# RWKV attention followed by a SwiGLU feed-forward block: a replanned static schedule with one fixed order of DMA issues

## The chip, the cores and the metric

One Trainium2 chip, one of its cores. The metric is the device time of one execution in microseconds (us): the median of repeated runs. A profiled execution adds a span, from the first to the last instruction, and a trace.

## What is computed

The first half is a recurrence over 768 steps for 4 batches of 8 heads with 48 channels:

```python
for t in range(S):
    cur = einsum('bhd,bhe->bhde', u[None] * kt, vt)
    y[:, :, t] = einsum('bhd,bhde->bhe', rt, state + cur)
    state = wt[:, :, :, None] * state + einsum('bhd,bhe->bhde', kt, vt)
```

Its output, 3,072 tokens of 384 channels, goes through a feed-forward network (FFN):

```python
xn = x / sqrt(mean(x * x) + 1e-06) * rms_g
g, val = xn @ w_gate, xn @ w_val            # 384 -> 1536
out = silu(g) * val @ w_out                 # 1536 -> 384
```

## The kernel before

**Tiling.** The 768 steps are cut into six superblocks, SB0 to SB5, of 128 steps. A superblock has four units, one per batch, each 128 tokens by 384 channels. Per unit, four loads of 192 KB bring w, k, r and v. The decays are summed by matmuls with masks (line 650), exponentiated on ScalarE (655) and multiplied into r and k on VectorE (658). The product is transposed, by TensorE (671) in SB0 and SB1 and by a DMA transpose (663) from SB2 on. Then come the scores (687), their mask on VectorE (690), the output (700, 703), the new state (709, 714, 721), the bonus term with u on GpSimd and VectorE (725, 729, 732, 737), the sum (741), the norm (745, 750, 751, 754) and a transpose into the FFN's input xnt (761, 765).

**FFN.** Per superblock, 12 blocks of 512 output columns in PSUM each for gate and value (line 774), silu on ScalarE (778), the product on VectorE (782), and 12 groups of four matmuls with w_out (790), whose result is copied (796, 798) and stored (802). Before the change, SB0 and SB1 run gate and value in two groups of two units (matmuls of 256 columns), the others in one group of four (512 columns). The gate and value weights arrive as 12 loads of 384 KB (606) in 7 staging buffers, 4 of which lie in the second `ht` buffer, and are scaled and cast to bf16 by ScalarE (614, gate) and VectorE (616, value). w_out comes in three DMAs that GpSimd issues (620).

**What sets the order.** Nothing is scheduled on the chip. `program` (line 218) lists every operation with engine, duration, dependences, ring buffers and a priority worked out from six target times `T`, and `Scheduler.run` (63) places them one by one: on each engine, among the operations ready soon, the one of lowest priority number. The order found is then issued as it is; each engine runs its own list in order and waits on semaphores. Loads and stores share the queue of SyncE (SP). Loads after a fixed first list (`LOADS`, 468) go out by priority; `in_w`, `in_rk` and `in_v` have two buffers per superblock parity, so a load for SB m waits until SB m-2 has been read. In the planner a DMA occupies SP for 0.55 us whatever is queued. ScalarE swaps its function table (624) 13 times.

Of the kernel before, what the change touches and what calls it, by code (L numbers as in the profile page):

```python
# [41 lines left out]
class Scheduler:  # L42


    DMA_RATE = {"in": 0.940 / 196608, "w": 1 / 330e3, "out": 0.60 / 196608, "tr": 1.0 / 262144}
# [7 lines left out]
    def op(self, name, eng, busy, fn, deps=(), prio=0.0, lat=0.0, alloc=(), nbytes=None, after=None):  # L53
        o = Op(name, eng, busy, lat, list(deps), prio, fn, [(r, k) for r, k, _ in alloc], nbytes)
# [8 lines left out]
    def run(self):  # L63
# [23 lines left out]
        dma_t = 0.0  # L87
        order = []
# [17 lines left out]
        while len(order) < n:  # L106
# [29 lines left out]
            o.slots = {}  # L136
            for r, k in o.alloc:
# [12 lines left out]
                else:  # L150
# [3 lines left out]
                    o.slots[k] = i  # L154
            o.start = ts
            free[o.eng] = ts + o.busy
            if o.nbytes is not None:
                kind, nb = o.nbytes
                st = max(ts + o.busy + 0.6, dma_t)
                dma_t = st + nb * self.DMA_RATE[kind]  # L160
                o.end = dma_t + 1.3
            else:
                o.end = ts + o.busy + o.lat
# [30 lines left out]
LOOK = 0.03  # L194

# [22 lines left out]
def program(S, T):  # L218
# [13 lines left out]


# [13 lines left out]
    for a, b in zip(LOADS, LOADS[1:]):  # L247
        before[b] = ("ldw",) + a[1:] if a[2] in "gh" else ("ld",) + a
    for m, j, w in seq:
# [43 lines left out]
    for m in range(NSB):  # L293
        t_le = T[0] - 30 if m == 0 else (T[0] + LE1 if m == 1 else T[m - 2] + (T[m - 1] - T[m - 2]) * LEFRAC)
        b = t_le
# [21 lines left out]
        for j in range(SB):  # L317
# [3 lines left out]
            if m == 0 or m == 1 and LE1SPREAD:  # L321
# [38 lines left out]
            S.op(("ruk2",) + u, POOL, 1.04, ("ruk2", m, j), [("ruk1",) + u], z - LAG["xa"] - 4.9, 0.03)  # L360
# [5 lines left out]
            S.op(("sq",) + u, ACT, act_t(DM, False, 0.18), ("x_sq", m, j), [("xa",) + u], z - LAG["sq"], 0.03)  # L366
# [25 lines left out]
    for m in range(NSB):  # L392
# [4 lines left out]
        for gi, (j0, nj) in enumerate(groups[m]):  # L397
            nf = 4 // nj
            nblk = FC // nf
            for i in range(nblk):  # L400
                fs = list(range(i * nf, (i + 1) * nf))
                frac = (i + 0.5) / nblk if INTERLEAVE else (sum(n for _, n in groups[m][:gi]) * 1.0 + nj * i / nblk) / SB
                t = T[m] + dur_gv * frac
                if m == 0:
                    t = T[0] + dur_gv * (i / nblk) + gi * HEADSP * nj
# [4 lines left out]
                xd = [("xe", m, j) for j in range(j0, j0 + nj)]  # L410
                for s, d in zip("gv", wdep):
# [3 lines left out]
                         [("bank", ("gvb", m, gi, i, s), rd)])  # L415
                ph = SIPH(m, gi, i)
# [10 lines left out]
            for j in range(j0, j0 + nj):  # L427
                for q in range(NOQ):
# [6 lines left out]
                    else:  # L435
# [3 lines left out]
                eng = OENG(m, j)  # L439
# [417 lines left out]
```

## Time and profile before

| | |
|---|---|
| median of 3 runs | 274.2 us (273.45 to 274.66) |
| the profiled execution | 271.89 us, span 269.8 us |
| mean granted TensorE clock, share of full | 0.956 |
| TensorE busy (matmuls) | 210.4 us, 78% |
| VectorE busy | 161.8 us, 60% |
| ScalarE busy | 135.0 us, 50% |
| GpSimd busy | 88.8 us, 33% |
| HBM read and written | 26.15 MB and 4.72 MB |

Busy time is a share of the whole span; where the time is lost is read per stretch, by which wait ends last there. In the rows, PE is TensorE, DVE VectorE, ACT ScalarE, POOL GpSimd, and a "q" behind an engine is its queue of DMA issues.

### The profile page before, as it was taken

To read this page: it belongs to the slowest core of one execution; us is meant where nothing else is said; L and a number is where in the kernel's file an instruction comes from. 1 tells how busy PE (TensorE), PEld (TensorE's weight loads), DVE (VectorE), ACT (ScalarE), POOL (GpSimd) and SP (SyncE) were. 2 spreads that over 40 slices of the span, in tenths; PEclk is the share of its full clock that TensorE was granted. 3 is DMA by queue.
4 is the path that set the end of the run, shared out by engine and by line. 5 is a ranking of instruction groups with operands and counts; after the bars stand their busy time and mean duration, and the time that the engine had idled before them with its cause. 6 is when DMAs were issued, how large, how long until landed. Compare 5 with 4: busy or idle time off the path is not lost.

```text
span 269.8 us, 4531 instructions
## 1 busy us (share of the span) xinstructions
PE 210.4 (78%) x1678; PEld 124.3 (46%) x1688; DVE 161.8 (60%) x273; ACT 135.0 (50%) x242; POOL 88.8 (33%) x133
## 2 busy tenths in 40 slices
PE   0476980577759895398989889978988888999984
PEld 0255760255526683185544436533454334554442
DVE  3479743457748572378985787684657647515521
ACT  2559652157163456547844439543486345533420
POOL 2566128634463570047632673120221011110000
PEclk9999999599798999579999999999999999999999
DMA  6999999999999967597999601920005800020002
GB/s 124 192 186 338 212 191 176 262 247 170 190 194 217 194 127 129 108 195 119 207 177 232 87 2 45 163 67 0 2 5 124 148 0 0 4 89 29 2 8 108
DMA packets 127142, 34.18 MB, mean 127 GB/s; under 512 B 117776, under 2 KB 127120, under 8 KB 127120
## 3 DMA queue, kind: packets, MB, share of 16 engines
q1 hardware_dynamic: 124992, 32.52, 64.4%
q0 software_dynamic: 1584, 1.18, 2.8%
q10 hardware_dynamic: 544, 0.20, 0.4%
q8 instruction: 13, 0.21, 0.4%
q14 instruction: 9, 0.07, 0.1%
HBM read 26.15 MB, written 4.72 MB: 114 GB/s over the span
## 4 chain that ended last, share of the span: by engine, by line
PE 44%; DVE 15%; SPq 13%; ACT 10%; DMA 7%; issue 6%; POOL 4%; DVEq 0%; ACTq 0%; POOLq 0%
PE ps L774 20%; PE ps L790 15%; SPq L593 12%; DVE ht L782 8%; ACT sg L778 5%; DMA in_v<-in_v_dram 4%; DMA in_rk<-in_r_dram 2%; PE ps L650 2%; SPq L606 2%; POOL ruk L725 1%; PE ps L687 1%; ACT ps L655 1%; DVE xb L741 1%; DMA in_w<-in_w_dram 1%; ACT vb L632 1%
## 5 line engine op out<-in xcount | busy, mean ns | idle before, releaser
L782 DVE TENSOR_TENSOR ht<-ps,sg 128x512 bf16<-128x512 f32 x72 | 49.2, 690 | 44.8 <-PE ps L774 27.0
L778 ACT ACTIVATE sg<-ps 128x512 bf16<-128x512 f32 x72 | 42.3, 597 | 59.1 <-PE ps L774 34.7
L774 PE MATMUL ps<-xnt,wv 128*128 128x256 bf16 (+1 forms) x286 | 59.9, 334 | 14.5 <-DVE wv L616 8.9
L774 PE MATMUL ps<-xnt,wg 128*128 128x256 bf16 (+1 forms) x280 | 60.1, 336 | 6.3 <-ACT wg L614 1.5
L790 PE MATMUL ps<-wo,ht 128*128 128x384 bf16 x288 | 55.4, 331 | 2.4 <-ACT xnt L765 0.9
L774 PEld LDWEIGHTS <-wv 128*128 128x128 bf16 x288 | 28.2, 100 | 36.8 <-DVE wv L616 11.6
L737 POOL TENSOR_TENSOR ydr<-in_v,diag 128x384 f32<-128x384 f32 x24 | 19.9, 830 | 61.7 <-DVE xb L741 52.9
L774 PEld LDWEIGHTS <-wg 128*128 128x128 bf16 x288 | 27.9, 102 | 24.9 <-issue 7.3
L790 PEld LDWEIGHTS <-ht 128*128 128x128 bf16 x288 | 26.7, 99 | 20.5 <-issue 5.5
L725 POOL TENSOR_TENSOR ruk<-in_rk 128x384 f32<-128x384 f32 x24 | 24.0, 999 | 25.8 <-DMA in_rk<-in_r_dram 23.3
L690 DVE TENSOR_TENSOR qts<-ps,mask_lt 128x1024 bf16<-128x1024 f32 x24 | 29.1, 1220 | 3.6 <-PE ps L687 3.4
L658 DVE TENSOR_TENSOR rkA<-in_rk,ps 128x768 bf16<-128x768 f32 x24 | 22.3, 950 | 13.2 <-ACT ps L655 13.1
L729 POOL TENSOR_TENSOR ruk<-ruk,u_bc 128x384 f32<-128x384 f32 x24 | 24.0, 1000 | 1.2
L655 ACT ACTIVATE ps<-ps 128x768 f32<-128x768 f32 x24 | 18.8, 794 | 9.2 <-PE ps L650 9.1
L750 POOL TENSOR_SCALAR rstd<-rstd 128x1 f32<-128x1 f32 x24 | 4.7, 198 | 53.2 <-ACT junk L745 52.5
L741 DVE TENSOR_TENSOR xb<-ps,ydr 128x384 bf16<-128x384 f32 x24 | 13.3, 554 | 9.8 <-PE ps L703 4.8
L650 PE MATMUL ps<-lw,mask_lt 128*128 128x384 bf16 x24 | 8.8, 366 | 12.8 <-ACT lw L627 7.9
L765 ACT COPY xnt<-ps 128x384 bf16<-128x384 bf16 x24 | 11.4, 480 | 14.7 <-PE ps L761 8.1
L624 ACT ACT_TABLE_LOAD x13 | 16.7, 1283 | 1.9 <-PEq L841 1.7
L732 DVE TENSOR_REDUCE diag<-ruk 128x8 f32<-128x384 f32 x24 | 13.1, 546 | 7.5 <-POOL ruk L729 7.4
L721 DVE TENSOR_TENSOR st<-ps,wcr 48x192 bf16<-48x192 f32 x40 | 14.0, 352 | 3.7 <-PE ps L774 2.3
L745 ACT ACTIVATE junk<-xb 128x384 bf16<-128x384 bf16 x24 | 12.4, 518 | 5.8 <-DVE xb L741 5.6
(49 smaller groups left out, 202.5 us busy)
## 6 DMA issues: line engine op xcount, KB each, us to landing
in_w<-in_w_dram SPq DMA_DIRECT2D x24, 192.0 KB, 4.2
in_rk<-in_k_dram SPq DMA_DIRECT2D x24, 192.0 KB, 4.6
in_rk<-in_r_dram SPq DMA_DIRECT2D x24, 192.0 KB, 4.6
in_v<-in_v_dram SPq DMA_DIRECT2D x24, 192.0 KB, 4.5
out_dram<-obr SPq DMA_DIRECT2D x24, 192.0 KB, 2.1
ht<-in_moe_w_val_dram SPq DMA_DIRECT2D x5, 384.0 KB, 5.0
ht<-in_moe_w_gate_dram SPq DMA_DIRECT2D x3, 384.0 KB, 5.4
stage_x<-in_moe_w_gate_dram SPq DMA_DIRECT2D x3, 384.0 KB, 5.9
```

The lines of the kernel that those rows point to most:

```text
L593: self.nc.sync.dma_start(out=t, in_=getattr(self, w)[j, :, m * L:(m + 1) * L, :].rearrange("h t d -> t h d"))
L624: self.nc.scalar.preload_act_table_set(LN_EXP if ph[0] == "le" else SILU)
L655: self.nc.scalar.activation(out=ps, in_=ps, func=AF.Exp)
L658: self.nc.vector.tensor_tensor(out=self.rkA[:, self.slot["rkA", m, j], :, :, 0:D], in0=self.in_rk[:, self.slot["in_rk", m], j], in1=self.b ...
L690: self.nc.vector.tensor_tensor(out=self.qts[:, self.slot["qts", m, j]].rearrange("p a q t -> p (a q) t"), in0=self.b2(("qb", m, j)).rearra ...
L725: self.nc.gpsimd.tensor_tensor(out=self.ruk[:, self.slot["ruk", m, j]], in0=rk[:, 0], in1=rk[:, 1], op=ALU.mult)
L729: self.nc.gpsimd.tensor_tensor(out=t, in0=t, in1=self.u_bc, op=ALU.mult)
L737: self.nc.gpsimd.tensor_tensor(out=self.ydr[:, self.slot["ydr", m, j]], in0=self.in_v[:, self.slot["in_v", m], j], in1=self.diag[:, m * SB ...
L774: self.nc.tensor.matmul(ps[:, i * n:(i + 1) * n], lhsT=w[:, c, f * 128:(f + 1) * 128], rhs=x[:, c], start=(i == 0 and c == 0), stop=(i == ...
L778: self.nc.scalar.activation(out=self.sg[:, self.slot[("sg",) + key]], in_=self.b1(("gvb",) + key + ("g",)), func=AF.Silu)
L782: self.nc.vector.tensor_tensor(out=self.ht[:, self.slot["ht", m], fs[0]:fs[-1] + 1, j0 * L:j0 * L + n], in0=self.b1(("gvb",) + key + ("v", ...
L790: self.nc.tensor.matmul(ps, lhsT=self.ht[:, self.slot["ht", m], f, j * L:(j + 1) * L], rhs=self.wo[:, f, :], start=(f == 0), stop=(f == FC ...
```

## The change

It replaces the planner's rules and its numbers; no arithmetic of the result changes.

- **One DMA order.** Every load waits, in the plan, for the issue of the load before it in one sequence: a new first list of 32 (all of SB0, all 12 weight loads, unit 0 of SB1), then w, k, r, v unit by unit. u and g move from ScalarE's queue into SP's, behind the sixth load.
- **Back pressure.** In the plan SP stays occupied until 1.3 us before its DMA starts to move; DMA rates and the TensorE's cold half-rate (`COLD`) are new.
- **Units.** Gate and value in SB0 run for units {0,1}, {2}, {3}, in SB1 for {0}, {1}, {2,3}: matmuls of 128 columns for the single ones.
- **Casts.** The 36 weight casts, 18 on ScalarE and 18 on VectorE before, are 12 each on ScalarE, VectorE and GpSimd.
- **Targets.** Priorities get an offset per stage and superblock (`OFF`); cuts of the silu phases, lags, the engines of copies (`OACT`, `TRE`) and the place of the w_out loads (`WODEP`) are new constants. 12 table loads instead of 13.
- **Aligned tiles.** `u_bc`, `g_col`, `wcr`, `diag`, `rstd` are allocated behind the large tiles. The address of `in_w` in a partition goes from 18080 to 16512, a multiple of 64, and the rings behind it likewise.

The core of the diff:

```diff
+        prio += OFF.get(name[:2] if name[0] in OFFKINDS else None, 0.0)
...
+            busy = o.busy
+            if o.eng == PE:
+                if o.name[0] == "gv":
+                    warm = True
+                elif not warm:
+                    busy *= COLD
+            free[o.eng] = ts + busy
             if o.nbytes is not None:
                 kind, nb = o.nbytes
-                st = max(ts + o.busy + 0.6, dma_t)
+                st = max(ts + o.busy + 0.3, dma_t)
                 dma_t = st + nb * self.DMA_RATE[kind]
-                o.end = dma_t + 1.3
+                o.end = dma_t + (1.3 if kind != "tr" else 1.5)
+                free[o.eng] = max(free[o.eng], st - 1.3)
...
-    for a, b in zip(LOADS, LOADS[1:]):
+    for a, b in zip(seq, seq[1:]):
...
-        p = i * 0.9 if m < 2 else T[m] - LOADLEAD + 0.01 * i
+        p = i * 0.9
...
+    S.op(("ldu",), SP, 1.0, ("load_ug",), (), 0.0, 0.0, (), ("in", 196608), [("ld",) + LOADS[UAFTER]])
...
-                eng = CASTENG(g, w, c)
+                eng = (POOL, DVE, ACT)[CASTENG[(g * 2 + "gh".index(w)) * KC + c]]
...
                 S.op(("od", m, j), SP, 0.55, ("o_dma", m, j), [("oo", m, j)],
-                     T[m] + dur_gv + (per - dur_gv) * (j + 1) / SB, 0.0, (), ("out", 196608))
+                     T[m] - 40, 0.0, (), ("out", 196608))
...
+GROUPS = {0: ((0, 2), (2, 1), (3, 1)), 1: ((0, 1), (1, 1), (2, 2))}
+CASTENG = (2, 2, 2, 1, 1, 1, 1, 1, 1, 0, 0, 0, 0, 0, 0, 2, 2, 2, 1, 1, 1, 1, 1, 1, 0, 0, 0, 2, 2, 2, 2, 2, 2, 0, 0, 0)
+WODEP = ((1, 0, 'r'), (1, 0, 'r'), (0, 3, 'v'))
...
-START, ITERS = [25, 54, 83, 112, 141, 170], 6
+START, ITERS = [-12.306, 1.745, 49.433, 100.66, 127.986, 152.461], 1
```

**SP's list, the weights.** In the list before, this is what stands from the seventh weight load to the eighth (lines 606 load weights; `in_w`, `in_rk`, `in_v` are unit loads of SB1 and SB2):

```order
L606 DMA stage_x<-in_moe_w_gate_dram 128x3x256
L593 DMA in_rk<-in_k_dram 128x8x48
L593 DMA in_rk<-in_r_dram 128x8x48
L593 DMA in_v<-in_v_dram 128x8x48
...
L593 DMA in_w<-in_w_dram 128x8x48
L593 DMA in_rk<-in_k_dram 128x8x48
L606 DMA ht<-in_moe_w_val_dram 128x3x256
```

13 unit loads stand between the two. In the list of the change, the same seventh and eighth weight loads (line 822) and the last ones:

```order
L822 DMA stage_x<-in_moe_w_gate_dram 128x3x256
L822 DMA ht<-in_moe_w_val_dram 128x3x256
L805 DMA in_rk<-in_k_dram 128x8x48
L822 DMA ht<-in_moe_w_val_dram 128x3x256
L822 DMA ht<-in_moe_w_gate_dram 128x3x256
L805 DMA in_v<-in_v_dram 128x8x48
L805 DMA in_w<-in_w_dram 128x8x48
L805 DMA in_rk<-in_r_dram 128x8x48
L822 DMA ht<-in_moe_w_val_dram 128x3x256
L805 DMA in_v<-in_v_dram 128x8x48
L822 DMA stage_x<-in_moe_w_gate_dram 128x3x256
```

All 12 weight loads now stand among the first 32 loads.

**SP's list, the end of the loads.** In the list of the change, the last loads of SB5 stand ahead of the DMA transposes (line 882) of SB4 and SB5:

```order
L805 DMA in_w<-in_w_dram 128x8x48
L1021 DMA out_dram<-obr 128x384
L805 DMA in_rk<-in_k_dram 128x8x48
L805 DMA in_rk<-in_r_dram 128x8x48
L805 DMA in_v<-in_v_dram 128x8x48
L1021 DMA out_dram<-obr 128x384
L882 DMA_TRANSPOSE rkT<-rkA 128x8x128 x2
L1021 DMA out_dram<-obr 128x384
L882 DMA_TRANSPOSE rkT<-rkA 128x8x128 x6
```

All 16 loads of SB5 stand ahead of SB4's transposes; ahead of SB3's first transpose stand five of SB4's loads.

**GpSimd's list in SB0.** With the change, casts (line 832) stand between the bonus and norm steps of units 2 and 3 (944, 948, 956 the bonus, 969 and 970 the norm) and ahead of the w_out loads (836):

```order
L956 TENSOR_TENSOR ydr<-in_v,diag 128x384
L832 TENSOR_SCALAR wv<-stage_x,g_col 128x256
L832 TENSOR_SCALAR wg<-stage_x,g_col 128x256 x3
L832 TENSOR_SCALAR wv<-stage_x,g_col 128x256 x2
L969 TENSOR_SCALAR rstd<-rstd 128x1
L970 TENSOR_TENSOR rstd<-rstd,mhalf 128x1
L832 TENSOR_SCALAR wg<-ht,g_col 128x256 x3
L956 TENSOR_TENSOR ydr<-in_v,diag 128x384
...
L836 DMA wo<-in_moe_w_out_dram 128x4x384 x2
```

Before, GpSimd's list held no cast.

## Rows read from the trace of the kernel before

**Rows 1.** Busy time by stretch (us; count in brackets), then granted clock, DMA share, GB/s.

```profile
0.00:26.90 26.90, 13.09 (x134) 8.95 (x135) 17.09 (x30) 15.62 (x30) 14.43 (x28) 1.00 1.08 209
26.90:61.50 34.60, 22.25 (x158) 16.16 (x158) 17.40 (x39) 15.76 (x33) 16.86 (x21) 0.90 1.17 215
61.50:87.40 25.90, 18.97 (x192) 12.00 (x191) 18.14 (x30) 11.75 (x23) 11.63 (x16) 0.87 1.14 195
87.40:137.50 50.10, 39.61 (x385) 28.25 (x384) 33.62 (x55) 29.86 (x49) 22.52 (x31) 0.90 0.90 156
137.50:176.90 39.40, 34.44 (x298) 18.34 (x300) 28.50 (x48) 21.79 (x37) 15.21 (x22) 1.00 0.63 117
176.90:210.70 33.80, 29.90 (x210) 14.86 (x209) 20.88 (x35) 18.64 (x33) 5.14 (x11) 1.00 0.19 37
210.70:241.60 30.90, 28.43 (x192) 14.08 (x196) 16.23 (x25) 14.06 (x28) 2.97 (x8) 1.00 0.17 38
241.60:269.80 28.20, 23.76 (x121) 11.72 (x120) 9.97 (x15) 7.53 (x13) 0.00 (x0) 1.00 0.11 42
```

**Rows 2.** Timeline of PE: start, us, [idle before, who ended it].

```profile
40.26 0.82 PE L774 MATMUL ps<-xnt,wg 128*128 128x256 bf16 x6
49.66 2.84 PE L774 MATMUL ps<-xnt,wv 128*128 128x256 bf16 x12 [8.59 <-DVE wv L616]
...
95.67 0.82 PE L774 MATMUL ps<-xnt,wv 128*128 128x256 bf16 x6
96.33 0.82 PE L774 MATMUL ps<-xnt,wg 128*128 128x256 bf16 x6
```

**Rows 3.** Timeline of SP's queue, 0 to 66 us.

```profile
0.73 0.46 SPq L593 DMA_DIRECT2D in_w<-in_w_dram  x1
...
13.68 4.09 SPq L593 DMA_DIRECT2D in_v<-in_v_dram  x4
17.82 0.95 SPq L606 DMA_DIRECT2D ht<-in_moe_w_gate_dram  x1
...
21.57 7.97 SPq L593 DMA_DIRECT2D in_w<-in_w_dram  x4
29.58 0.71 SPq L606 DMA_DIRECT2D stage_x<-in_moe_w_gate_dram  x1
...
52.53 0.44 SPq L606 DMA_DIRECT2D ht<-in_moe_w_val_dram  x1
...
60.95 4.89 SPq L593 DMA_DIRECT2D in_v<-in_v_dram  x2
```

**Rows 4.** Timeline of ACT at the start of SB1.

```profile
73.13 0.51 ACT L632 CAST vb<-in_v 128x384 bf16<-128x384 f32 x1 [7.34 <-DMA in_v<-in_v_dram]
```

**Rows 5.** DMA issues: KB of one, median us from issue to landing.

```profile
in_v<-in_v_dram SPq DMA_DIRECT2D x24, 192.0 KB, 4.5
ht<-in_moe_w_val_dram SPq DMA_DIRECT2D x5, 384.0 KB, 5.0
wo<-in_moe_w_out_dram POOLq DMA_DIRECT2D x3, 384.0 KB, 8.6
```

**Rows 6.** The line of the DVE casts: min/median/max ns, first and last start.

```profile
L616 DVE TENSOR_SCALAR wv<-ht,g_col x15: 334/348/675, 28.0 to 59.9; 128x256 bf16<-128x256 f32 x15
```

**Rows 7.** Timeline of DVE: casts beside an idle GpSimd, and beside a busy one.

```profile
28.01 1.14 DVE L616 TENSOR_SCALAR wv<-ht,g_col 128x256 bf16<-128x256 f32 x4
...
54.67 1.20 DVE L616 TENSOR_SCALAR wv<-ht,g_col 128x256 bf16<-128x256 f32 x3 [0.38 <-DMA ht<-in_moe_w_val_dram]
```

**Rows 8.** Group of GpSimd's multiplications of r and k.

```profile
L725 POOL TENSOR_TENSOR ruk<-in_rk 128x384 f32<-128x384 f32 x24 | 24.0, 999 | 25.8 <-DMA in_rk<-in_r_dram 23.3
```

**Rows 9.** Timeline of PE: eight 128-column matmuls, each with its own weights.

```profile
66.20 0.62 PE L671 MATMUL ps<-ident,rkA 128*128 128x128 bf16 x8
```

**Rows 10.** SP's own waits at its DMA transposes and at loads (us, times, longest).

```profile
SPq L663 <- DVE rkA L658: 9.7, 8, 2.7
SPq L593 <- ACT lw L627: 9.3, 2, 5.9
```

More of the change, by code (lines that the diff above doesn't have):

```diff
@@ L86, in run @@
                 pend[o.eng].append(o)
-        dma_t = 0.0
-        order = []
+        dma_t, warm = 0.0, False
+        order, last = [], {}
         INF = 1e9
@@ L231, in tgt @@
         return T[m] - 1.0 - (SB - 1 - j) * (HEADSP if m == 0 else STEADYSP)
+    blocks = []
+    for m in range(NSB):
+        per = (T[m + 1] - T[m]) if m + 1 < NSB else 28.0
+        for gi, (j0, nj) in enumerate(groups[m]):
+            nblk = FC * nj // 4
+            for i in range(nblk):
+                first = sum(n for _, n in groups[m][:gi])
+                if m == 0:
+                    t = T[0] + per * 2 / 3 * (i / nblk) + gi * HEADSP * nj
+                elif INTERLEAVE:
+                    t = T[m] + per * 2 / 3 * (i + 0.5) / nblk
+                else:
+                    t = T[m] + per * 2 / 3 * (first + nj * i / nblk) / SB
+                blocks.append((m, t, gi, i))
+    blocks.sort()
+    siph, btime = {}, {}
+    for n, (m, t, gi, i) in enumerate(blocks):
+        siph[m, gi, i] = ("si", sum(c <= n for c in CUTS))
+        btime[m, gi, i] = t
+    le_at = {m: blocks[CUTS[m]][1] + LEOFF[m] for m in range(1, NSB)}
     loads = []
@@ L320, in program @@
             dt = m in DMATR
-            if m == 0 or m == 1 and LE1SPREAD:
+            if m == 0:
                 tc_ = z - LAG["cs"]
@@ L443, in program @@
                 S.op(("od", m, j), SP, 0.55, ("o_dma", m, j), [("oo", m, j)],
-                     T[m] + dur_gv + (per - dur_gv) * (j + 1) / SB, 0.0, (), ("out", 196608))
-    for i, ph in enumerate(PHASES):
-        prev = phase.get(PHASES[i - 1], []) if i else []
+                     T[m] - 40, 0.0, (), ("out", 196608))
+    order = []
+    for k in range(NSB):
+        order.append(("le", k))
+        if ("si", k + 1) in phase:
+            order.append(("si", k + 1))
+    for i, ph in enumerate(order):
+        prev = phase[order[i - 1]] if i else []
         first = min(S.by[x].prio for x in phase[ph])
-        S.op(("tab", ph), ACT, 1.283, ("table", ph), list(prev) + ([("tab", PHASES[i - 1])] if i else []), first - 1.3, 0.0)
+        if i and order[i - 1][0] == ph[0]:
+            S.op(("tab", ph), ACT, 0.0, ("nothing",), list(prev) + [("tab", order[i - 1])], first - 1.3, 0.0)
+        else:
+            S.op(("tab", ph), ACT, 1.283, ("table", ph), list(prev) + ([("tab", order[i - 1])] if i else []), first - 1.3, 0.0)
 NSTAGE, NWG = 7, 6
```

256 lines of the change are left out of this document (216 added, 40 removed), and 3 rows, old and new, of the table LOADS.

## The prediction, made before the change was run

> **What bounds the kernel now.** I read the busy time of the engines in eight stretches first [rows 1]. The cuts lie at the first gate matmul of SB0 (26.9 us), the end of SB0's gate and value (61.5), and the first gate matmuls of SB1 (87.4), SB2 (137.5), SB3 (176.9), SB4 (210.7) and SB5 (241.6). The reader is to see two different kernels. From 137.5 to 241.6 TensorE is busy 92.8 of 104.1 us (34.44 + 29.90 + 28.43) and the DMA engines are mostly idle (117, then about 37 GB/s). Before 87.4 us TensorE is busy 54.3 of 87.4 us, while the DMA engines move 195 to 215 GB/s. So the first third is bound by what the DMA queue brings and in which order, the rest by TensorE with VectorE close behind.
>
> The timeline of TensorE shows the worst hole: gate matmuls end at 41.1 us, and the next value matmuls start at 49.66 after 8.59 us of idleness that a weight cast ended [rows 2]. The timeline of SP's queue says why: seven weight loads are out by 29.58 us, but the last one goes out only at 52.53, behind unit loads of SB1 and SB2 [rows 3]. The same queue then sends two of SB1's v loads at 60.95, and ScalarE waits 7.34 us for a v until 73.13 [rows 4]. Both holes are matters of order, not of bytes.
>
> **A yardstick.** To compare stretches with different matmul widths I count columns in the instruction order. Blocks of 1,536 columns follow each other every 0.66 us when nothing waits (95.67 to 96.33) [rows 2]. By that, the program before holds about 22.7 us of TensorE work up to 61.5 us, 47.9 from there to SB2's first gate matmul, 85.3 from there to SB5's, and 24.6 in the last stretch. The program of the change holds, between the same marks, 22.9, 47.7, 85.0 and 25.3. Work over time is then 0.63 in 61.5 to 137.5, 0.82 in 137.5 to 241.6 (85.3 in 104.1).
>
> **The change, part by part.**
>
> *The weights move forward.* Everything up to the last weight load is 20 unit loads, u, and 12 weight loads. Sixteen unit loads took from 0.73 to 17.82 us, 1.07 us each, those in the backlog 1.0 [rows 3]. From 17.82 to 29.58 the queue took six weight loads and four unit loads: 11.8 less 4.0 leaves 1.3 us a weight load [rows 3]. So the last weight load leaves at 0.7 + 20 x 1.0 + 1.0 (u) + 11 x 1.3 = 36 us, lands 5.0 later [rows 5], and its three casts take 3 x 0.35 [rows 6]: the last weights are ready at 42.1. I allow six gate or value blocks behind them, 4 us: SB0's gate and value end at 46 instead of 61.5, **15.5 us earlier**. Bytes agree: 8.9 MB by 41 us are 215 GB/s, the rate of the two first stretches [rows 1]. Of the tiles' new alignment no row tells anything. Below, its price is nothing, the pace staying 1.0 us; above, a unit load could at best go at a weight load's rate per byte, half of 1.3 us, 7 us off for 20. I take zero, since nothing in the rows ties the pace to an address.
>
> *The casts on GpSimd.* Twelve of 128x256, of which no row exists. From below a VectorE cast, 0.35 us [rows 6]; from above GpSimd's two-input product of 384 columns, 1.0 us [rows 8]. I take that by columns, 0.67: 8 us in all. GpSimd is busy 16.9 of 34.6 us between 26.9 and 61.5 and 14.4 of 26.9 before [rows 1], so idle time covers them. If that cover is gone, the norms of units 2 and 3 and the w_out loads queue behind casts, up to 8 us. Behind w_out wait SB0's output matmuls: issued near 40 us and landing 8.6 later [rows 5], it is ready near 49, some 3 us after SB0's gate and value end. Masks and products of SB1 fill this in part; it is in the range, not in the sum.
>
> VectorE's casts took 0.285 us each next to an idle GpSimd and 0.40 next to a busy one, the longest 0.675 against 0.334 [rows 6, 7]. For 12 casts that remain the worst is 12 x 0.34 = 4 us, and VectorE is busy only 17.4 of 34.6 us there, so it costs nothing in the sum. The Trainium skill (SBUF — State Buffer, "Who interferes with whom") says that VectorE and GpSimd share one pair of SBUF ports as an exclusive lock: a `tensor_scalar` in a two-port mode blocks GpSimd, or is blocked, for a whole instruction. By that rule, casts on both engines at once would be one line of casts, and adding GpSimd would not help. The trace agrees that casts lengthen beside GpSimd, though not that they stop; the rule makes a rival below.
>
> *Units.* In SB0 and SB1, 144 matmuls and as many weight loads are added; the columns stay. Eight matmuls of 128 columns, each with its own weights, take 0.62 us including one fill of about 0.3 [rows 9]: under 0.055 us each, which is 128 columns at 2.4 GHz. Cost: zero; from above, 144 x 0.05 = 7 us if the weight loads were not covered. One table load less is 1.3 us of ScalarE, hidden.
>
> *SB1 and the way to SB2.* Behind the last weight load come 12 more unit loads of SB1 and three w_out loads: 12 x 1.0 + 3 x 1.3 = 16 us, landing at 57 us. SB1's units are then there one after another between 41 and 57, and TensorE starts them at 46: the wait for v [rows 4] is gone. What is late next is the chain of VectorE and ScalarE through each unit, as in the later superblocks. So I take their ratio, 0.82, for the 47.7 us of work: 58 us, SB2's first gate matmul at 104 instead of 137.5. That is **18 us more**. The granted clock, 0.87 and 0.90 in these stretches against 1.00 later [rows 1], is inside that ratio.
>
> *SB2 to SB5.* The work is the same (85.0), so at 0.82 it is 103.7 us. TensorE's idle time here is 104.1 - 92.8 = 11.3 us [rows 1]. The new plan puts SB3's output matmuls between SB4's gate matmuls and brings SB2 to SB5 new priorities. Ends: all 11.3 come back, or none (or as much is lost). I take 5, less than half, for lists that are in order on two engines above 60% cannot both be filled. The last stretch, 25.3 us of work against 24.6 in 28.2, takes 28.9.
>
> **Sum.** 46 + 58.2 + 98.7 + 28.9 = 231.8 us of span. The profiled execution stood 2.1 us above its span: 233.9. It lay 0.8% under the median of the three runs (271.89 against 274.2), so I forecast **235 us** for the median, 14% less. A change of 0.5% is about what can be told from none.
>
> **The rivals.**
>
> *Only the weights move (255 us).* The 15.5 us come, but SB1 still goes at 0.63: in the plan every stage hangs on small offsets, and one late operation stalls a whole in-order engine. Against: the two waits named are removed by the order itself. 235 + 18 + some of the 5 gives 255. Chance 0.14.
>
> *Everything fits (221 us).* SB1 runs at 0.90 (53 us, 5 less) and SB2 to SB5 get all 11.3 back (6 less), 3 us from faster loads. For it: TensorE reaches 0.92 busy in 210.7 to 241.6 [rows 1]. Chance 0.14.
>
> *One line of casts (240 us).* Casts on VectorE and GpSimd exclude each other: 12 x 0.34 on VectorE, and the rest through later w_out loads, 5 us before SB1. The Trainium skill's rule on the shared ports (SBUF — State Buffer, "Who interferes with whom") is this one. Chance 0.07.
>
> *The fixed queue holds up the transposes: slower (283 us).* SP works in order, and all of SB5's 16 loads stand ahead of SB4's DMA transposes, five of SB4's ahead of SB3's. A load of SB m needs SB m-2's buffers, v's last reader being GpSimd's bonus step. If that is late, the scores of a whole superblock wait behind 16 loads at 1.0 us: 16 us each for SB3, SB4 and SB5, 48 in all, 235 + 48. Before, transposes waited for their own data, 9.7 us in eight waits, and loads for ScalarE's read of w, up to 5.9 us [rows 10], which shows that loads do stand in SP waiting for buffers. Against: the DMA engines have room from 137 us on. It decides from 13 us per superblock, where three eat the gain. Chance 0.05.
>
> **How the numbers follow.** The forecast's own case has 0.60, between 224 and 246. The range takes in the clean case and the case of the weights alone, **219 to 256**, and leaves out the slow rival and the far ends. Faster by over 0.5%: 0.60 + 0.14 + 0.14 + 0.07 = 0.95, less 0.02 for the ends: 0.93; within 0.5%: 0.01; slower: 0.06.
>
> **What would show it.** Right: the last weight load leaves SP near 36 us, SB0's gate and value end near 46, no wait of TensorE above 3 us on a weight cast, SB2's first gate matmul at 100 to 108, about 99 us from there to SB5's. The weights step is wrong if the last value matmul of SB0 is later than 52; the SB1 step if SB2 starts after 115; the steady step if SB2 to SB5 takes over 107. The forecast as a whole falls if SP's list of waits shows loads waiting over 10 us for GpSimd with transposes behind them.

## The result, and the profile after

The changed kernel takes **245.59 us** (median of 4 runs, 244.13 to 246.18) against 273.82 before: ratio **0.8967**, 95% interval 0.8908 to 0.9026. Forecast were 235 us and a range of 219 to 256. The direction, the place of the gain and the range held; the forecast was 10.6 us short. The profiled execution took 244.13 us, its span 242.4; it is the fastest of the four.

Busy time by stretch, changed kernel, columns as in [rows 1]. The cuts are the first gate or value matmul of SB0, the end of SB0's gate and value, and the first gate matmuls of SB1 to SB5:

```profile
0.00:23.80 23.80, 10.32 (x98) 6.74 (x99) 12.81 (x25) 13.06 (x22) 13.61 (x26) 1.00 0.96 210
23.80:50.30 26.50, 21.82 (x269) 17.80 (x267) 18.81 (x34) 16.62 (x35) 20.45 (x25) 1.00 1.06 234
50.30:66.20 15.90, 13.30 (x144) 8.71 (x142) 11.65 (x19) 7.87 (x17) 6.34 (x9) 1.00 0.81 169
66.20:111.16 44.96, 39.20 (x499) 29.31 (x499) 36.96 (x62) 31.07 (x53) 23.95 (x34) 1.00 0.95 190
111.16:145.57 34.41, 32.35 (x263) 17.77 (x267) 27.72 (x46) 23.00 (x38) 22.17 (x29) 1.00 1.03 207
145.57:171.07 25.50, 23.90 (x193) 12.50 (x196) 22.09 (x38) 18.31 (x30) 10.09 (x16) 1.00 0.32 62
171.07:209.28 38.21, 33.81 (x230) 16.44 (x233) 18.99 (x29) 14.85 (x32) 2.95 (x8) 1.00 0.16 43
209.28:242.40 33.12, 27.68 (x132) 12.71 (x131) 11.56 (x18) 7.64 (x13) 0.00 (x0) 1.00 0.12 42
```

Up to SB2's first gate matmul the way took 137.5 us; now it takes 111.2. Of the 27.4 us of span that are gained, 26.3 lie there. The granted clock reads 1.00 in every stretch of this execution; before, it was 0.87 to 0.90 from 26.9 to 137.5. The other three executions of the changed kernel had 0.990 to 0.992 and took 245.25 to 246.18 us. It does not hold for the start: as the rows of TensorE below show, six matmuls of 256 columns take 1.48 us at 23.81 and 0.82 at 28.65, so TensorE starts at about half the pace.

SP's queue in the changed kernel (start, us), the answer to [rows 3]:

```profile
33.65 0.53 SPq L822 DMA_DIRECT2D stage_x<-in_moe_w_gate_dram  x1
...
54.38 0.67 SPq L805 DMA_DIRECT2D in_v<-in_v_dram  x1
```

The last weight load leaves at 33.65 us instead of 52.53, SB1's last v at 54.38 instead of 60.95 or later. ScalarE's wait for a v [rows 4], 7.34 us, is down to 0.4.

TensorE from SB0's gate and value on, the answer to [rows 2]:

```profile
23.81 1.48 PE L993 MATMUL ps<-xnt,wv 128*128 128x256 bf16 x6
...
28.65 0.82 PE L993 MATMUL ps<-xnt,wv 128*128 128x256 bf16 x6
...
42.93 2.35 PE L993 MATMUL ps<-xnt,wg 128*128 128x128 bf16 x30 [1.07 <-ACT sg L997]
...
46.62 0.83 PE L993 MATMUL ps<-xnt,wg 128*128 128x128 bf16 x12 [0.67 <-DVE ht L1001]
...
49.53 0.83 PE L993 MATMUL ps<-xnt,wv 128*128 128x128 bf16 x12 [0.74 <-DVE ht L1001]
...
111.16 0.81 PE L993 MATMUL ps<-xnt,wg 128*128 128x512 bf16 x2 [0.57 <-ACT xnt L984]
```

The hole of 8.59 us behind a cast is gone. In its place, TensorE waits at the end of SB0 for silu and for the product of gate and value.

In the last stretch the wait for the product comes in every pair of blocks. TensorE and VectorE there (two views of the changed kernel):

```profile
218.16 0.81 PE L993 MATMUL ps<-xnt,wv 128*128 128x512 bf16 x3
218.80 0.81 PE L993 MATMUL ps<-xnt,wg 128*128 128x512 bf16 x3
219.82 0.81 PE L993 MATMUL ps<-xnt,wv 128*128 128x512 bf16 x3 [0.20 <-DVE ht L1001]
...
221.48 0.81 PE L993 MATMUL ps<-xnt,wv 128*128 128x512 bf16 x2 [0.21 <-DVE ht L1001]
```

```profile
219.07 0.69 DVE L1001 TENSOR_TENSOR ht<-ps,sg 128x512 bf16<-128x512 f32 x1 [0.97 <-PE ps L993]
```

A pair of gate and value blocks takes 1.66 us (219.82 to 221.48), seven times in a row. The timeline of the kernel before has a gate block every 1.30 us in its last stretch:

```profile
242.88 0.81 PE L774 MATMUL ps<-xnt,wg 128*128 128x512 bf16 x3
...
244.18 0.81 PE L774 MATMUL ps<-xnt,wg 128*128 128x512 bf16 x3
```

The value block at 219.82 starts when the product from 219.07 is done, and that product reads the value block of 218.16. In the plan the two value blocks have *different* PSUM banks, 1 and 0. They are the two halves of one PSUM tile (`ps0`, 128x2x512). In the plan of the kernel before, the blocks of its last stretch take all eight banks in turn; in the changed plan the last 20 blocks have four, 2 and 3 for gates, 1 and 0 for values.

### The profile page after: what moved, and what is told of

It is laid out like the page before. It is cut to its first block, busy times and chain, and to the rows that moved or that the text cites. A ratio compares the mean times of both kernels' runs of the same rounds, so it can differ in the third digit from the quotient of the medians.

```text
span 242.4 us, 4821 instructions
## 1 busy us (share of the span) xinstructions
PE 202.4 (84%) x1820; PEld 122.0 (50%) x1832; DVE 160.6 (66%) x266; ACT 132.4 (55%) x236; POOL 99.6 (41%) x145
## 3 DMA queue, kind: packets, MB, share of 16 engines
q1 hardware_dynamic: 125536, 32.71, 62.4%
## 4 chain that ended last, share of the span: by engine, by line
PE 44%; DVE 18%; ACT 10%; SPq 8%; issue 7%; DMA 6%; POOL 5%; DVEq 0%; POOLq 0%; ACTq 0%
PE ps L993 24%; PE ps L1009 12%; DVE ht L1001 8%; SPq L805 5%; ACT sg L997 5%; DVE rkA L877 3%; DMA stage_x<-in_moe_w_gate_dram 3%; SPq L822 2%; POOL wg L832 2%; DVE xb L960 2%; PE ps L906 2%; DVE xnr L973 2%; ACT junk L964 2%; DMA in_w<-in_w_dram 2%; DMA in_rk<-in_r_dram 1%
## 5 line engine op out<-in xcount | busy, mean ns | idle before, releaser
L993 PE MATMUL ps<-xnt,wv 128*128 128x128 bf16 (+2 forms) x357 | 59.0, 295 | 5.8 <-DVE ht L1001 3.7
L993 PE MATMUL ps<-xnt,wg 128*128 128x128 bf16 (+2 forms) x351 | 58.4, 296 | 6.2 <-ACT sg L997 1.9
L1009 PE MATMUL ps<-wo,ht 128*128 128x384 bf16 x288 | 54.1, 326 | 1.9 <-DVE ht L1001 1.3
L993 PEld LDWEIGHTS <-wv 128*128 128x128 bf16 x360 | 29.2, 98 | 25.6 <-issue 10.4
L993 PEld LDWEIGHTS <-wg 128*128 128x128 bf16 x360 | 28.9, 99 | 23.2 <-issue 9.0
L1009 PEld LDWEIGHTS <-ht 128*128 128x128 bf16 x288 | 26.9, 97 | 20.8 <-issue 3.0
L909 DVE TENSOR_TENSOR qts<-ps,mask_lt 128x1024 bf16<-128x1024 f32 x24 | 28.9, 1217 | 0.7 <-PE ps L906 0.4
L874 ACT ACTIVATE ps<-ps 128x768 f32<-128x768 f32 x24 | 18.8, 795 | 3.7 <-PE ps L869 3.3
L984 ACT COPY xnt<-ps 128x384 bf16<-128x384 bf16 x24 | 11.4, 478 | 11.5 <-PE ps L980 7.5
L1017 ACT COPY obr<-ps 128x384 f32<-128x384 f32 x10 | 4.8, 478 | 18.7 <-PE ps L1009 15.6
```

Source lines behind the costliest of these rows:

```text
L874: self.nc.scalar.activation(out=ps, in_=ps, func=AF.Exp)
L909: self.nc.vector.tensor_tensor(out=self.qts[:, self.slot["qts", m, j]].rearrange("p a q t -> p (a q) t"), in0=self.b2(("qb", m, j)).rearra ...
L993: self.nc.tensor.matmul(ps[:, i * n:(i + 1) * n], lhsT=w[:, c, f * 128:(f + 1) * 128], rhs=x[:, c], start=(i == 0 and c == 0), stop=(i == ...
L1009: self.nc.tensor.matmul(ps, lhsT=self.ht[:, self.slot["ht", m], f, j * L:(j + 1) * L], rhs=self.wo[:, f, :], start=(f == 0), stop=(f == FC ...
```

## The experiments

The theory behind the prediction: the order of loads gives SB0, SB1 follows with the later superblocks' ratio of work to time, alignment and GpSimd's casts cost nothing. Marks of every run's profiled execution, read from TensorE's timeline (us; "B" is built on the kernel before, "A" on the changed one):

| kernel | median | ratio to before | SB0's gate/value end | SB2's first gate | SB5's first gate | span |
|---|---|---|---|---|---|---|
| before | 273.8 | 1 | 61.5 | 137.5 | 240.1 | 269.8 |
| b_bp: B, one line on SP | 262.9 | 0.963 (0.959 to 0.968) | 50.0 | 130.1 | 232.4 | 262.1 |
| b_bpu: b_bp and units | 261.5 | 0.954 (0.947 to 0.961) | 52.2 | 124.0 | 227.8 | 257.5 |
| a_rules: new rules, old numbers | 256.9 | 0.941 (0.937 to 0.945) | 53.8 | 122.2 | 228.5 | 256.7 |
| a_nobp: A without the line on SP | 264.4 | 0.966 (0.959 to 0.973) | 50.8 | 127.4 | 229.4 | 262.5 |
| a_off0: A without offsets | 255.6 | 0.934 (0.927 to 0.940) | 51.1 | 112.2 | 220.2 | 252.8 |
| **changed kernel (A)** | 245.6 | 0.897 (0.891 to 0.903) | 50.4 | 111.2 | 209.3 | 242.4 |
| a_nopool: A, no casts on GpSimd | 247.7 | 0.904 (0.897 to 0.911) | 54.4 | 115.2 | 213.6 | 246.6 |
| b_aligned: B, aligned tiles | 269.3 | 0.987 (0.981 to 0.992) | 61.8 | 135.8 | 238.4 | 268.1 |
| a_unaligned: A, old addresses | 245.4 | 0.901 (0.897 to 0.906) | 51.6 | 112.4 | 210.5 | 243.6 |
| a_tail: A, banks of SB5 | 241.9 | 0.889 (0.884 to 0.893) | 50.3 | 113.7 | 211.8 | 241.6 |
| a_banks: A, banks of SB0, 1, 4, 5 | 239.3 | 0.876 (0.873 to 0.878) | 48.1 | 110.2 | 205.4 | 237.1 |
| a_banks_un: a_banks, old addresses | 239.4 | 0.875 (0.873 to 0.878) | 50.6 | 112.3 | 207.5 | 239.2 |
| a_tiles: A, tiles in turn | 238.5 | 0.873 (0.868 to 0.877) | 48.2 | 111.1 | 207.8 | 237.4 |

SB5's first gate block of the kernel before stands at 240.1 us; the mark of 241.6 in the prediction was its first value block. The runs come from several chips; each ratio is to the kernel before on the same chip, and where two medians lie close, the ratios with their intervals decide.

### b_bp: one line of the planner alone

```diff
                 o.end = dma_t + 1.3
+                free[o.eng] = max(free[o.eng], st - 1.3)
```

> The kernel before with one line added to its planner: SP stays occupied until 1.3 us before its DMA starts to move. Nothing else changes; the planner makes new lists, in which the last weight load stands behind 20 unit loads instead of 46. Theory (the order of the loads is what the first half of the gain is): last weight load out at 34 to 37 us, SB0's gate and value end at 46 to 51 instead of 61.5, SB1 follows as far as its offsets allow: 250 to 256 us, ratio 0.91 to 0.935. Rival (the gain hangs on the offsets and the units, the order alone only closes the two named holes): 262 to 268 us.

SP's queue of this run:

```profile
32.64 0.51 SPq L607 DMA_DIRECT2D ht<-in_moe_w_val_dram  x1
```

The last weight load leaves at 32.64 us and SB0 ends 11.5 us earlier, as the theory had it. But the time is the rival's, 262.9: at SB2 7.4 us are left, since the way from SB0's end to SB2 now takes 80.1 us (50.0 to 130.1; 76.0 before). The line is worth 10 us. It moves more than the loads: the planner makes all lists anew, so the order of the loads by itself has no run.

### b_bpu: the units on top of it

```diff
-GROUPS = {0: ((0, 2), (2, 2)), 1: ((0, 2), (2, 2))}
+GROUPS = {0: ((0, 2), (2, 1), (3, 1)), 1: ((0, 1), (1, 1), (2, 2))}
```

> The kernel before with the one line on SP's occupation and the new units: gate and value in SB0 for units {0,1}, {2}, {3}, in SB1 for {0}, {1}, {2,3}; priorities and engines as before. Compared with the one line alone (262.9 us, SB1's first gate matmul at 74.5 us, SB2's near 130). Theory (units let SB1's gate start when its first unit is ready and fill TensorE): SB1's first gate matmul before 70 us, SB2's at 120 to 125: 254 to 258 us. Rival (the units only help where priorities are made for them): 262 to 264 us.

SB1's first gate matmul comes at 69.0 instead of 74.5 us and SB2's at 124.0, as the theory said. The median falls by only 1.4 us (ratios 0.963 and 0.954, intervals that overlap), nearer to the rival. The 144 added weight loads make no loss in the total, as predicted, though SB0 ends 2.2 us later than in b_bp. In the profiled executions the granted clock differs too, 0.94 instead of 0.89 between SB0's end and SB2, and TensorE is busy 57.7 instead of 61.6 us there.

### a_rules and a_nobp: rules without numbers, numbers without a rule

a_rules removes the block of new constants (lags, `LOADS`, units, casts, cuts, `OFF`) and takes the old starting targets; a_nobp removes one line from the changed kernel:

```diff
-LAG = {'cs': 13.821,
...
-START, ITERS = [-12.306, 1.745, 49.433, 100.66, 127.986, 152.461], 1
+START, ITERS = [25, 54, 83, 112, 141, 170], 6
```

```diff
-                free[o.eng] = max(free[o.eng], st - 1.3)
```

> The planner's rules of the change (fixed sequence, SP's occupation, DMA rates, cold TensorE, aligned tiles, u and g on SP) with the numbers of before: old lags, load list, units, casts, targets, no offsets. Theory (rules and numbers share the gain; the rules bring the weights forward as the one line on SP did, 262.9 us, and the aligned tiles some 2 to 4 us): 256 to 261 us. Rival (the numbers only polish): 250 us or less. Second rival (rules without numbers made for them are worth nothing beyond the one line): 262 to 266 us.

> The changed kernel without the line that keeps SP occupied in the plan until 1.3 us before its DMA starts to move; the loads keep their fixed sequence. Theory (the fixed sequence holds the load order whatever the plan thinks of SP, so the line no longer decides): 246 to 250 us, last weight load out at 33 to 36 us. Rival (the plan must know when data lands to order the compute lists): SB0 to SB2 come apart again, over 254 us, with stores or transposes in front of loads in SP's list.

a_rules came as its theory had it, 256.9. a_nobp fell to its rival, **18.8 us slower** than the changed kernel, though its loads leave in the same fixed sequence and the last weight load at 34.6 us. TensorE and ScalarE of a_nobp behind SB0 (two views):

```profile
56.65 0.48 PE L868 MATMUL ps<-lw,mask_lt 128*128 128x384 bf16 x1 [5.83 <-ACT lw L845]
```

```profile
55.66 0.51 ACT L850 CAST vb<-in_v 128x384 bf16<-128x384 f32 x1 [4.43 <-DMA in_v<-in_v_dram]
56.08 1.76 ACT L845 ACTIVATE lw<-in_w 128x384 bf16<-128x384 f32 x4
```

Without the line the plan believes that SB1's third v can be cast at 43.5 us, and that w_out lands at 57 to 65 us (43 to 49 with the line). So on ScalarE that cast stands ahead of SB1's logarithms and waits until 55.66, and on TensorE SB1's masks, which need the logarithms, stand ahead of SB0's output matmuls: 5.83 us of nothing. The order of the loads does not need the line; the compute lists do. The other numbers of the change were made for a plan that has the line, so what is lost without it here, 18.8 us, holds for these numbers and not for any plan.

### a_off0: the offsets

```diff
-OFF = {('bs', 0): 1.553,
...
+OFF = {}
```

> The changed kernel with its table of offsets per stage and superblock emptied; loads, units, casts, lags, cuts and the planner's rules stay. Theory (what took SB1 from 76.0 to 60.9 us is the order of loads, the units and the lags; the offsets only polish): 247 to 250 us, near the 3 us by which the plan gets longer. Rival (the schedule hangs on the offsets; one late operation stalls a whole in-order engine): over 254 us.

The time went to the rival, 10 us slower, but not where it looked for it. At SB2's first gate a_off0 is 1.0 us behind the changed kernel; from there to SB5's it needs 108.0 us instead of 98.1. Busy time of a_off0 from 66.00 us on, shortly before SB1's first gate matmul:

```profile
66.00:112.15 46.15, 39.69 (x502) 31.29 (x503) 35.95 (x61) 30.69 (x53) 22.17 (x33) 0.96 0.93 188
112.15:220.17 108.02, 91.99 (x707) 47.75 (x704) 69.60 (x114) 56.89 (x100) 37.04 (x55) 1.00 0.47 99
```

TensorE is busy 92.0 us here and 90.1 in the changed kernel, so 8.0 of the 9.9 us are idle time, in many waits of about a microsecond. Two of the longest:

```profile
115.72 0.81 PE L848 MATMUL ps<-xnt,wv 128*128 128x512 bf16 x3 [1.47 <-ACT sg L852]
...
180.17 0.81 PE L848 MATMUL ps<-xnt,wg 128*128 128x512 bf16 x3 [1.39 <-DVE qts L764]
```

### a_nopool: the casts of GpSimd on VectorE

```diff
-        eng = (POOL, DVE, ACT)[CASTENG[(g * 2 + "gh".index(w)) * KC + c]]
+        eng = (DVE, DVE, ACT)[CASTENG[(g * 2 + "gh".index(w)) * KC + c]]
```

(in the emission alone; the plan stays)

> The changed kernel with the same lists, only the 12 weight casts of GpSimd are issued on VectorE, at the same places of the order. Theory of the prediction (idle time covers GpSimd's casts, though they take 0.92 us and not 0.67): taking 11.1 us off GpSimd and putting 12 x 0.35 = 4.2 us on VectorE leaves the time at 245.6 us within 1 us. Rival, the one line of casts: casts on the two engines hold each other up, so that with all of them on VectorE the weights are ready 2 to 5 us sooner and SB0's gate and value end by 47 instead of 50.3 us: 241 to 243 us. Second rival: VectorE is what paces SB0 (products behind casts), so the 4.2 us show: 248 to 250 us.

SB0's gate and value end 4.0 us later and the profiled span is 4.2 us longer; the median, 2.1 us higher, does not tell this from no change (0.8969 to 0.9109 against 0.8908 to 0.9026). The second rival is nearest, and the one line of casts is out: it asked for a gain. In the changed kernel, a line of GpSimd's casts (min/median/max ns), VectorE's timeline with the casts at 30.91 beside GpSimd's, and GpSimd's there:

```profile
L832 POOL TENSOR_SCALAR wg<-stage_x,g_col x3: 922/922/922, 27.8 to 29.6; 128x256 bf16<-128x256 f32 x3
```

```profile
17.74 0.88 DVE L832 TENSOR_SCALAR wv<-ht,g_col 128x256 bf16<-128x256 f32 x3
...
30.91 1.22 DVE L832 TENSOR_SCALAR wv<-ht,g_col 128x256 bf16<-128x256 f32 x3
```

```profile
30.53 1.90 POOL L832 TENSOR_SCALAR wv<-stage_x,g_col 128x256 bf16<-128x256 f32 x2
```

Three VectorE casts went through in 1.22 us beside two GpSimd casts of 0.95 us each: 0.41 us each instead of 0.29 at 17.74, as before [rows 6, 7], and GpSimd's 3% longer than 0.92. The Trainium skill (SBUF — State Buffer, "Who interferes with whom") has one of the two engines blocked for the whole instruction of the other, where a VectorE instruction in a two-port mode meets GpSimd; beside casts these rows show a slowing by 0.11 us a cast, and no such block.

Beside GpSimd's products of two tensors the block does show. VectorE's normalisation (`xnr`, a `tensor_scalar`) takes 0.32 us alone, and 0.88 where it starts inside such a product (VectorE and GpSimd, changed kernel):

```profile
18.83 0.32 DVE L973 TENSOR_SCALAR xnr<-xb,rstd 128x384 bf16<-128x384 bf16 x1 [0.21 <-POOL rstd L970]
...
39.85 0.88 DVE L973 TENSOR_SCALAR xnr<-xb,rstd 128x384 bf16<-128x384 bf16 x1 [0.37 <-POOL rstd L970]
```

```profile
39.78 0.83 POOL L956 TENSOR_TENSOR ydr<-in_v,diag 128x384 f32<-128x384 f32 x1
```

It ends 0.12 us behind the product. Six of the 24 normalisations start inside a `ydr` or `ruk` product; they take 0.39 to 1.05 us, and each ends 0.11 to 0.12 us behind it. The longest cast of the kernel before [rows 6], 0.675 us, is of this kind: it is the first of the three at 54.67 [rows 7], and GpSimd was in a product until 55.20:

```profile
54.37 0.83 POOL L737 TENSOR_TENSOR ydr<-in_v,diag 128x384 f32<-128x384 f32 x1 [1.19 <-DVE diag L732]
```

The other two of the three took 0.34 us each beside a GpSimd that had stopped. So the prediction's "0.40 next to a busy one" is the mean of one cast held up and two free ones.

That idle time covers GpSimd's casts, as the theory has it, is not shown. In the changed kernel the chain that ended last (start and us) lies on GpSimd from 27.83 to 36.88 us, and eight of its casts make 6.96 us of that:

```profile
27.83 2.72 POOL wg L832 x3
...
36.07 0.81 POOL ydr L956
36.90 0.57 DVE xb L960
```

```profile
37.50 0.60 ACT L997 ACTIVATE sg<-ps 128x512 bf16<-128x512 f32 x1 [1.30 <-DVE xb L960]
```

A unit's bonus product (`ydr`) stands behind the casts, its sum (`xb`) waits for it, and ScalarE is idle 1.30 us before a silu, which the profile puts down to that sum. What a_nopool shows is that the same casts cost more on VectorE, not that they are free on GpSimd.

### a_unaligned, b_aligned, a_banks_un: the addresses

The edit moves `u_bc`, `g_col`, `wcr`, `diag`, `rstd` ahead of the large tiles again (or, in b_aligned, behind them), and nothing else:

```diff
+        self.u_bc = const.tile([128, H, D], FP32, name="u_bc")
+        self.g_col = const.tile([128, KC], FP32, name="g_col")
...
-        self.wcr = ring("wcr", [SB, NP], FP32)
```

> The changed kernel with the same lists, its five small tiles put back where they were, so that in_w and the rings behind it lie at 18080 instead of 16512. Theory of the prediction (alignment priced at zero): 245.6 us within 0.5%, the last weight load leaves at 33.7 us, unit loads land after about 4 us. Rival (the alignment makes transfers faster): unit loads in the backlog take 1.0 us instead of 0.85 to 0.9 and land after 4.5 us, the last weight load leaves near 36 us, and the whole is 2 to 7 us slower, 248 to 252 us.

> The kernel before with its lists as they are, only the five small tiles behind the large ones (in_w at 16512). Theory (alignment is worth nothing): 273.8 us within 0.5%, the first 16 unit loads out at 17.8 us as before. Rival: the first 16 unit loads are out by 15 to 16 us and in_v lands after 3.8 instead of 4.5 us; the order of the weight loads stays, so that 2 to 5 us of it show: 269 to 272 us.

> The kernel with the changed bank rule, with the tiles at the old, unaligned addresses, to price the alignment beside the aligned one on one chip. Theory (the changed kernel has slack in its loads; the first gate matmul comes 1.2 us later, and nothing else): 1 to 1.5 us slower than the aligned one. Rival, from the kernel before, where aligned tiles gave 3.7 us: 3 to 4 us slower. Second rival: no difference within 0.5 us.

Loads at 16512 are faster. The queue of loads (packets, MB, its share of 16 engines' span) and a load's landing, in a_unaligned, then in the changed kernel:

```profile
q1 hardware_dynamic: 125536, 32.71, 69.4%
...
in_v<-in_v_dram SPq DMA_DIRECT2D x24, 192.0 KB, 4.5
```

```profile
q1 hardware_dynamic: 125536, 32.71, 62.4%
...
in_v<-in_v_dram SPq DMA_DIRECT2D x24, 192.0 KB, 3.8
```

In b_aligned the landing is 3.9 us instead of 4.5 [rows 5]. The queue's own time per DMA engine falls from 64.4% of 269.8 us to 56.9% of 268.1 (174 to 153 us) in the kernel before, and from 69.4% of 243.6 to 62.4% of 242.4 (169 to 151 us) in the changed one: a tenth and more for the same bytes. In the kernel before this is worth 1.3% (0.8% to 1.9%). In the changed kernel the last weight load leaves 1.3 us earlier and the profiled spans differ by 1.2 us, but the medians do not tell them apart: 245.4 and 245.6 (ratios to before 0.901 and 0.897, intervals that overlap), and with the better banks 239.42 and 239.30 on one chip, nearest to the second rival of a_banks_un. The price is small, at most about 1 us. The 1.2 us between the spans are already there at SB0's first gate or value matmul (24.97 against 23.81) and do not grow behind it: there the loads have slack. In b_aligned the first 16 unit loads are out at 16.6 us, between the theory's 17.8 and the rival's 15 to 16; the time is the rival's.

### a_tail, a_banks, a_tiles: who holds the value blocks up

The planner picks, among free banks, one whose neighbour in the tile is taken. a_tail and a_banks drop that preference for gate and value blocks of SB5, or of SB0, SB1, SB4 and SB5 (a_tail: `k[:2] != ("gvb", 5)`):

```diff
-                    i = min(c, key=lambda i: (banks[i ^ 1] <= ts, banks[i]))
+                    i = min(c, key=lambda i: (banks[i ^ 1] <= ts and not (k[0] == "gvb" and k[1] in (0, 1, 4, 5)), banks[i]))
```

a_tiles prefers, for the same blocks, a tile both of whose banks are free, the longest first:

```diff
+                    full = sum(max(banks[2 * p], banks[2 * p + 1]) <= ts + 1e-9 for p in range(4))
+                    if k[0] == "gvb" and k[1] in (0, 1, 4, 5) and full >= 2:
+                        i = min(c, key=lambda i: (banks[i ^ 1] > ts, max(banks[i], banks[i ^ 1]), banks[i]))
```

> The changed kernel with the same lists, but SB5's gate and value blocks take the PSUM bank that has been free longest, so that all eight banks take turns instead of four. Theory: in the changed kernel each value block waits 0.20 us for a product on VectorE because its bank was read only just before; with eight banks a pair of blocks takes 1.30 us instead of 1.66, some 8 pairs, so 2.6 to 3.0 us less: ratio to the changed kernel 0.988, about 242.7 us. Rival: the pace is set by silu and product themselves, or the last products and output matmuls set the end anyway: 245.6 us, pairs still 1.66 us.

> The changed kernel with the bank that has been free longest for the gate and value blocks of SB0, SB1, SB4 and SB5; all but three neighbouring entries of the lists stay. Theory (bank turnover costs 3.2 us in SB5, and the waits of 0.67 and 0.74 us on a product between 46 and 51 us are the same thing in SB0): SB0's gate and value end at 48.5 to 49.5 instead of 50.3 us, 240 to 241.5 us. Rival (SB0 is paced by silu and product, not by banks): SB0's end stays at 50 us, and the time that of the run with SB5 alone, 241.9 us.

> The changed kernel, same lists entry for entry; a gate or value block of SB0, SB1, SB4 and SB5 takes the PSUM tile (a pair of banks) that has been wholly free longest, as long as two tiles are free. Theory (waits go by the tile and not by the bank: a value block waits for the product that reads the other bank of its tile, and a silu for the value block written beside its gate): the two waits of 0.91 us that the bank rule left in SB5, at 215.7 and 222.0 us, vanish, pairs of blocks follow every 1.30 us, and SB0, SB1 and SB4 win a few tenths each: 236.5 to 238 us. Rival (waits go by the bank, and the two waits have another cause): 239.3 us as with the bank rule, the waits still there.

By the medians all three gain: 3.7, 6.3 and 7.1 us. By the ratios it is 2.2, 5.8 and 6.6 us, and a_tail's interval (0.884 to 0.893) still touches the changed kernel's (0.891 to 0.903), the two others' do not. In a_tail the last stretch takes 29.8 us instead of 33.1. In a_banks SB0 ends at 48.1 instead of 50.4, and the median is better than its theory had it. Two waits stay there (TensorE, a_banks):

```profile
213.99 0.81 PE L993 MATMUL ps<-xnt,wg 128*128 128x512 bf16 x3
215.71 0.81 PE L993 MATMUL ps<-xnt,wv 128*128 128x512 bf16 x3 [0.91 <-DVE ht L1001]
...
220.24 0.81 PE L993 MATMUL ps<-xnt,wg 128*128 128x512 bf16 x3
221.96 0.81 PE L993 MATMUL ps<-xnt,wv 128*128 128x512 bf16 x3 [0.91 <-DVE ht L1001]
```

Both value blocks have bank 0, read last over 4 us before, and wait for a product that reads bank 1, the other half of the tile. With whole tiles in turn both waits are gone and ten pairs in a row take 1.30 us each (TensorE, a_tiles):

```profile
212.52 0.81 PE L999 MATMUL ps<-xnt,wg 128*128 128x512 bf16 x3
...
213.81 0.81 PE L999 MATMUL ps<-xnt,wg 128*128 128x512 bf16 x3
...
224.82 0.81 PE L999 MATMUL ps<-xnt,wv 128*128 128x512 bf16 x3
```

So the wait goes by the tile. It comes from the program: in the trace the first matmul of the block waits on the semaphore that the product raises. The Trainium skill (PSUM — Partial Sum Buffer, "PSUM bank collisions raise a hardware error") asks for a guard per bank, and by that rule the block in bank 0 need not wait. a_tiles is the best kernel here, ratio 0.873; its lead over a_banks, 0.8 us, lies within the intervals, and its median came half a microsecond above what was expected.

## Why the prediction was right, and where it was off

**Weights forward (46 predicted, 50.4 came).** The order was right: last weight load out at 33.65 us (36 predicted), last weights cast at 41.7 (42.1 predicted). The step that failed is "six gate or value blocks behind them, 4 us". Seven and a half stood behind the last cast and took 8.7 us, 1.16 us each instead of 0.66. The turn of the PSUM banks is 2.3 us of the 4.4 (a_banks: 48.1). The rest has no run of its own; GpSimd's casts, next, are the likeliest part.

**Alignment, casts, units at nothing.** For the sum alignment (about 1 us at most) and units (no loss) held. The reason given for alignment, "nothing in the rows ties the pace to an address", was true of the rows and not of the chip: the aligned loads are faster, and the small price is slack in the loads, which the prediction did not argue. For the casts the step "so idle time covers them" failed. GpSimd's casts took 0.92 us instead of the estimated 0.67 [rows 8], 11.1 us in all, and eight of them lie on the chain that ended last, ahead of a unit's bonus and norm. The prediction names this case ("If that cover is gone") and keeps it out of the sum. Eight casts at 0.25 us more than priced are 2.0 us, an estimate of what the size alone can have cost; no run tests it.

**SB1 (58.2 predicted, 60.8 came).** Right in size, SB2's first gate at 111.2, inside the bound of 115 but outside 100 to 108. That the order of the loads would carry it, as the prediction has it ("the wait for v [rows 4] is gone"), was too simple. b_bp has the weights ahead in the same way and loses in SB1. It takes the units (6 us more at SB2, b_bpu), the planner's knowledge of when data lands (a_nobp, 16 us at SB2) and the other new numbers (122.2 in a_rules; a_off0 has 112.2, so it is not the offsets here). These prices overlap, and among the new numbers only the offsets were tried by themselves. Of the 15.1 us between the two profiles here (76.0 to 60.9), TensorE's busy time gives 6.1 (58.6 to 52.5 for the same columns, granted clock 0.89 to 1.00), idle time 9.1. The prediction kept the clock inside its ratio and so had no term for it; that the ratio 0.82 came near the 60.8 us is in part luck.

**SB2 to SB5 (98.7 predicted, 98.1 came).** The sum held, its reason in part. Between equal marks, the first gate matmuls, the stretch went from 102.6 to 98.1 us: 3.2 us of idle time (11.3 to 8.1) and 1.3 of busy time, where the prediction had 5 of idle time. And the 4.5 us are two terms: without offsets the new plan is slower here than the old one (108.0 against 102.6), and the offsets bring 9.9.

**The last stretch (28.9 predicted, 33.1 came).** The mis-sized term: it was priced by columns alone, with the old turn of PSUM tiles. The new plan's turn makes pairs of blocks take 1.66 us, which a_tail gives back (29.8). Some 1.5 us of the 4.2 are the mark: 24.6 us of work, counted from the first gate block, was set against 28.2 us, counted from the first value block, where 29.7 belongs to it. The same 1.5 us made the stretch ahead too long, so in the sum they cancel, and that too is luck.

4.4, 2.6 and 4.2 us late and 0.6 early make the 10.6 us by which the span, 242.4, missed 231.8. (The last step of the sum, from 233.9 to the median, is 0.8%: 235.9, not 235.)

**The rivals.** Slower by SP's queue: no. The rows of loads behind GpSimd come to 10.1 us in 16 waits, just at the 10 us that the prediction named as its sign, but none of the waits is longer than 1.7 us; what waited 17.3 us was a transpose, for its own data. SP's waits in the changed kernel, columns as in [rows 10]:

```profile
SPq L882 <- DVE rkA L877: 22.7, 5, 17.3
SPq L805 <- POOL rstd L969: 2.9, 3, 1.7
```

"Only the weights move" was put at 255 us; measured by b_bp that case is 262.9. "Everything fits" asked for 221; the best kernel here, with whole tiles in turn, comes to 238.5. "One line of casts" asked for a gain without GpSimd's casts, and a_nopool has none.

## What to carry to other kernels

In a planned schedule, the model of the queue sets the order of the *compute*: one line that tells the plan when data lands was worth 10 us alone and 19 us inside the finished plan, whose numbers had been made with it. That an engine is idle half of the time does not price work on it at nothing: look what stands behind that work in its list. Price a stretch with its buffers' turn, not by work alone: before trusting a sum of columns, look which buffer each block takes and what else lies in the same tile. And part a gain by stretch before naming its cause; the same total can hold one term that loses and another that gains.

## What was not expected of the hardware

**Destination addresses set the DMA's pace.** Rows of 192 bytes into partitions at 16512 instead of 18080 (a multiple of 64 against 32 beyond one) cost a tenth less queue time, unit loads landing in 3.8 instead of 4.5 us. Which multiple it takes is not shown: 16512 is a multiple of 128 too.

**The granted clock differs from run to run on the same lists.** From SB1's gate to SB2's, the changed kernel and a_tail have the same lists entry for entry. Busy time of the changed kernel there stands above (44.96 us, clock 1.00); a_tail:

```profile
66.10:113.67 47.57, 42.03 (x499) 31.63 (x499) 37.66 (x62) 31.22 (x53) 23.88 (x34) 0.93 0.91 185
```

A mean of 0.93 is part of the stretch at the lower of the two levels, 1.2 instead of 2.4 GHz. It costs 2.6 us, more than several of the edits. a_unaligned shows the same on one chip with one kernel: four executions with a mean of 1.000 took 244.9 to 245.4 us, two with 0.986 took 247.3. In a_nobp the clock falls in the 5.83 us in which TensorE stood idle, and behind them TensorE works at the lower level:

```profile
56.65:64.20 7.55, 6.53 (x58) 4.54 (x57) 4.59 (x8) 5.85 (x10) 5.40 (x7) 0.50 1.06 212
```

So a hole costs more than its length here. a_tail has no such hole. From 64 to 69 us TensorE is busy 1.9 of 5.0 us in the changed kernel and in a_tail alike, with the same waits; in a_tail the clock falls at the end of it, in the changed kernel it does not (changed kernel, then a_tail):

```profile
64.00:69.00 5.00, 1.95 (x24) 1.33 (x23) 4.85 (x9) 3.07 (x5) 3.25 (x6) 1.00 0.90 182
```

```profile
64.00:69.00 5.00, 1.92 (x25) 1.34 (x24) 4.85 (x9) 3.07 (x5) 3.25 (x6) 0.93 0.96 190
```

In a_off0, a_banks, a_banks_un and a_tiles it falls in these microseconds too, between 65 and 70. What decides, with the same work in front, stays open.

**GpSimd's products hold VectorE up.** A `tensor_scalar` that starts inside a product of two tensors ends 0.11 to 0.12 us behind it (0.88 us at 39.85 instead of 0.32, above); beside GpSimd's casts it is only slowed.
